# A spectral filter followed by a two-matmul block on one Trainium2 core: the table of issue order and engines is laid out anew

## The chip, the cores and the metric

The kernel runs on one core of a Trainium2 chip. Its time is the device time in microseconds of one execution; the time of a kernel is the median of several executions. Before the change it is 836.34 us, the median of three runs (835.13 to 836.74).

## The reference

```python
X = np.fft.rfft(x, axis=1)                  # x: 8 x 3008 x 256
Yr = Xr @ w_r - Xi @ w_i + b_r              # 256 x 256 weights
Yi = Xr @ w_i + Xi @ w_r + b_i
Yr, Yi = soft_threshold(Yr, 0.01), soft_threshold(Yi, 0.01)
y = np.fft.irfft(Yr + 1j * Yi, n=3008, axis=1)

h = y.reshape(24064, 256) @ w_in            # 256 x 2048
g = s * np.maximum(h, 0) ** 2 + b
out = g @ w_out                             # 2048 x 256
```

## The kernel before

The Fourier transform of 3008 = 94 x 32 points is done as two smaller transforms by matmuls. For each batch there are these steps, each a list of small units that are strewn between the matmuls of the second block:

- `s1_units`: the transform of length 94 (input `x16`, loaded by POOL in `load_x_later`, L360). The result `u` leaves PSUM by ACT or DVE (L301) and is written to a scratch tensor in HBM by the SyncE queue (SP, L796), and read back in another layout as `us` (`take_rows`, L812).
- `s23_units`: `fwd_unit` (transform of length 32, result `xf`), `sum_unit` (`s`) and `mix_unit` (the weights, result into `ring`, L889), then `shrink`: three DVE operations for the soft threshold (L908, L912, L916) and four moves on SP that bring the two halves of the partitions together (`ring<-ring`, L927; for the last units of a batch they are DVE copies, L933). `inv_unit` multiplies the moved `ring` by `T_t`; its result `v` is written to HBM (L964) and read back as `vs` in four loads of 384 KB (`take_half`, L981).
- `s4_units`: the last transform of length 94, into `yt`.

The second block runs over 48 tiles of at most 512 tokens. `first_mm` multiplies `yt` by `w_in` into PSUM (`psh`), 16 chunks of the 2048 columns for each tile. Two chunks at a time, ACT or DVE makes `relu` (`rt`, L1140 or L1142) and `square` (`gt`, L1151 or L1153). While a tile's first product runs, the tile before it gets its second one: `seven_mms`, a 2 x 2 block product with seven products in place of eight, into `psa`, or `second_mms` (plain) for the first four and last two tiles and those that are not full. The seven products need sums of the blocks of `gt`, in two halves q of the chunks: `s_op` with n = 1, 3 and 2 on DVE (L1303) and n = 4, `a12 = a12 + a11`, either on DVE (L1303) or as a transfer that POOL issues and that adds on its way (`gt<-gt`, L1295). DVE gathers the results (L1368) into `ost`, and SP sends them out (L1177).

What is not a matmul is recorded as a piece, in the order in which the program makes it. All 2681 pieces of the main part have an entry in the string `TURNS`: two base-36 digits make a number; its remainder by 4 is the engine (ACT, DVE, SP, POOL), its quotient a shift. `plan_turns` sorts the pieces by their place plus this shift, and `pump`, which runs ahead of each matmul, issues them in that order. So the table sets the engine of each piece and the order of each of the four queues. Each queue works its instructions strictly in that order. The order of the matmuls is not in the table: it follows from the calls.

```python
at = [divmod(int(TURNS[k : k + 2], 36), 4) for k in range(0, len(TURNS), 2)]
queue.extend(
    (k, ("act", "dve", "sp", "pool")[at[k][1]])
    for k in sorted(range(len(at)), key=lambda k: k + at[k][0])
)
```

Of the kernel before, what the change touches and what calls it, by code (L numbers as in the profile page):

```python
# [23 lines left out]


TURNS = (
    "24253220251x20281w262d1p29303a1o2942465i421c1t19181c211l181s1t34141t1w1g2p4b571b470r4310141s"
    "1930141o28191m221015191d1l1l1s2024301s2l1t2121292u3a2u26102d181l1p292l2x4u3m3u2q0w2o1h2m1q0s"
    "141h143w1d1x2d2d3u2i2y5e0o0x151p21293q2y4u220c2s0k0t10291o3k41111d1h2l5i4y46320812111c3w0x46"
    "162x0k0p0x191d1t3y1u422a08103s210k3q0p0s2o590s210p3q111h1x2p3u2q3a3u0c0g1s0l11151x212956463u"  # L30
    "2y0h0w1k2d2q3u051u0k1g1s0t2l0o6i1d1x292l463i2u2y0w1s0j370d0w1l0x1g381d1h1p1x3226362a0w321018"
    "2w3h4y5m3m4u0t15151l31213h39002y0h0g310p0x151h391p1h1l0c2i0g0g2t1c2i1g1s1h1x2y242c2x363a3e3e"
    "181g191m3a323u5a0x20113e0x10112c101g2c1d222m1c1m19291s241p21251w2k1w221s291t264e292l1s2k1p1v"
    "1s2w251l1o23251p1s2x1t21211q1w241x24242p21213m1x1w2h1t211s2d2m3q1k1o1x1k1s3a242o1t1y261c2p31"
    "1h1h3k1t1c1s2x3l242d1g2t1t191a1v1x1c2g1t1w1w2529351w2821291r731t1w281t2p1o1x1x2u2a1u4u1h212d"
    "2t4m4y5a360s1g140v5f1c1s111u2e12160p1h1l1x0t0w3k151r141t141o1p151t292h313i463q2u1b190s1t141h"
    "1o1t1c2x1p1o281p1s1n7f1t252l1s1w353h1p5e4a1h1p1x2h3i2m4y460o0w0x12101g0x2u1q0s212l103x143c0p"
    "130t1s3c1t110s101v1x1h2l142h1g761h1p292d2l2y3q3e2u1c25104614182c15181t184918201p39153i1x263e"
    "19181l15182x1c1k1w1h1m2u0z47212h1531393t4e4u3u4a0o280x0w4a104e0z0w1o0x0p0s131h151c1g281l191g"
    "1x1h252h2t4x31314d4d2t3p3p0o6q1d1m0k0w0l1d0s10281h491l561m2m1u0k0u0k2h0p1p1y1c241h221q2y2214"  # L40
    "252t1d1c2c1t1c1q3m3m2h2o320s241l0x2t1h18211p1d1k2h264m282e1k201l2120281x2d241p3i361l1s1t221o"
    "241l1u2q2d31191h3k251g2b1k1s3o291l1s2b211k1o2p1t1x201u1x341s20242w1t211u1x1w1x2s292x1p294e4m"
    "1h1k2c1h4a2e1g281d1i1m252x1d2s1h1g253p1c1p1g2s210x0y231t212k1o1x212l1o241x2125242c2121252d2h"
    "323q2i363b8319181c1s1h1p142p213m2y2e52150w1o0z5r191l1k201h3i2a2i1e151d1h253e263i3y152h0o1428"
    "1p0k2l1z0p0s2w1p0l0s2v1t18291c2d1l2h2l353y3a463e151c5i1828181c1h183c1d176r1d1h1g201h1p1g1t4y"
    "1s251h1s1l1t212d2y2i422u181i1g200p2m0s2h3918450t381d111r1414202l1p192p142b211h2l2x353a3u423a"
    "0o5y1024151e1h0w141w181h1p2q1s281h1p1p1x212h2t453l493135393d3h0w0w3o0x1p0w1m0f4z0l0u0g5i0k2x"
    "0o181k2c1p2u1d1m2l311d1d6e1k3c1h141e3i3q1f1c1g1o1p111s221j191h2g1s1l1t2h1o3e1u4e1o291l1o1t1k"
    "1w252h1g1q1h3m1o2g1t1s211p2i1k1u292p2438251d1c271s2030291t1t2b211k212t1w25251u202l1x20202c1x"
    "204e291x1w2c212p1p292u1k1p2k1k1q1y1o251p22292l1s3k211s3123282h1g391x1l1e1z211g2c1x1w1x24242x"  # L50
    "242g1t1x1z631t2c341p1x1o1x1x3u1t1x292h322m3i3u101w150z4v141s113a15291t290x1c2s0x1b1g251k301x"
    "1d1x29393t4e4i4u3q1719101x141d1d21181c1d1g201l1k1b5r251h251g201d1x294i1t21292l3m4m2q2y101819"
    "3m181o151e101x2h1545181s0x1b1d2445291p1c1t23291o1x1o201t3y1t1x21252p2y3e3m46141g143a1c1o2s15"
    "141d1h351c1t1d391c222h2m1h1g1s1l242l1p242c213m1n4j292p1p3d3p414m564q3y182c0p0o0y0x1a0v0w2419"
    "0t0w1b1t15141o2c1x1h1k341p1x252h2x4d4p3t31253l290s160w3m0w1w0x151c1d1l2x391l1y1446101o101l2q"
    "202k1p1y1c2h2x1o1h381p1o1y3q3u3d2d4e142l1h111n1d14201l1d1g2h2a1i282e1g201h21242o21291w1x3a1w"
    "2d1x2i1s2g1p1u2p311k1p3h1x1o231o1w38251p1s271x1o1w2s1w1x251u21291w24242g25251u252821292p351s"
    "25321o1o201p2u1u1w281l1u2h2l243g1l1p2l3p242l1g2t1t1h1a1v1x1g241t20212p2c2p1s241p1p3j7b211o20"
    "2h2p1k1p1x5e1h2d2l2p3q2u3y2y0o1c0w0r57141k113610291p2h0x14280t1714211c2o1t0x1t2d2x2x4a3e3m2u"
    "13150w2h0x1d142x181g1h1o28211o1j5n291x2h1s201t1x2h4y1t292h2l2u323i4i10140x4e141k112m101l2p18"  # L60
    "1p1g2x0l1319283g1x15181g1z2d1w211s2h1w3u1t1t252d2l3q2q3a3q181o1852141k2h151d1h1g351k2019211k"
    "3q252e1l1k1s1h1x31251o241l1u1j4f292l1l2p353h3u424m460w2811104e0w3y0z0w1s150t0s171p11181k281t"
    "1d1g391l1t252l354h3135412t353x0s3a0w160s140p1910141x2x3d193m141i181w1c1t1y242o1t221g2l311s1l"
    "2s1t1s263m3q1n2s2y1c241p193d1l1c1p211d1k2o2e461k1u1k2c1l1x1x241x25281t3a1s2d1t221o2c1l222p31"
    "1k1t401t1s231o282w251p1g2b1x1o1s2s1t1x211u253c1s21202c1x201u291x1w2s1x212a1w1w291x2q5u1w251t"
    "1u1w251w2921251o2h461s1s1t1s1x1w2h1s201p1r7r1p563q3a1i2q1m1k2w111h0w151d1l21292u3m2a460o210w"
    "0r57181s152q1q141l1t29111c3c1h1z1c211g1w1x1h252t31353q423246130t0w1g0x151h2l1c1g1l1o2g1l1w1j"
    "7b1p1x2920281p1x2d4i1t1t212t3i2u3i4a141g181i191k1d36101p291c351c3k0p17191s2t211d141h23211g2t"
    "1g311o661t1t1x253d4i563y4i101w145m14181k15191p1929181o0x29143u111a11181o191l2d211o241926174j"
    "2d2p1h3d3p454m52424m1c3c0l0o1q0x1a0v0w1g190t0w1b1t1514183k1x1h1k1w1p252d2t3x3d452x413p2x210p"  # L70
    "1e0s120o280x1d14182w192d1p4i195q1c2d1o1p2e242g1h1q1c2d2t1o1h341l1k1y3e3m1f2k2u142g1h111l1d14"
    "2w2p191d1p224i2c2m1g2g1h1p1t2o21291g1t221o2h1x261w2k1l1y2p2t1o243o1l1p1v1w202g291t1t2b211k21"
    "2s1w25251u21301w2120291x1w3i211s21342h3h1o1p2y1l1k1s1h261m1l241t262d2l20341p2o2x1r1o251o3121"
    "1l1e232121301x1w2021202h1w2g1t1t21252c252p1s212p3i1t1x2d2x42323e42101c141g1s1d1i191p2d2x1l1k"
    "2o1h1v1g2d1o2c251h252h31394e3a3m3q1f1d1k1s141d1d1h1k251h1k241l1o2d1x2h1s241x2l21261x292p4t5e"
    "5q5u4m181g1h221c1w191e1c1t291g3d1k200x1719182g1h151d1f1p182514381l1t212d314i4q3i2y101c1d3i1c"
    "1o1919211d1l1c1s25351d1q1h1o201p1x2d20281p3a2d2l1t2l31394m3i463m141k0t141i0v1k201l151g1r1p1x"
    "1o251t1s202821252d2h2t2l3d2t2h3p352x242i0s100p150w2c1h2h253i142d1h282e1o201l262h311p1s2s1p1w"
    "2a3a3q1n1k2k1x1d1z1p1s281p1t21223e1w251x251w21292t1x221k1w242h1t222p311s203w1x1k231o282w251p"
    "1g27291t1k2k1o1x1x292l1t202c3d1t1s21251w2k1w1x2y1s1s2d1p2q1w2d1l1u1w2g20202125242524242h463e"  # L80
    "4a2m2a361d1g191l1c1x1g1w1h321i21291o34191n1s2l211p271t1s2821252c202d1x212429212l29361s1s1x20"
    "212a292l1s2g1h2t1s30211l271x1o20212125242o2121202k1x1x21361x2021241x262h2p1w301h1r1w2x211p27"
    "1x1o2c1x1w2k202p1x1x1w212h2m1s1x1w21292a1w24252524252425242l213e2i22262q2e1c29191t1k291w243d"
    "3m3a21251o281d1n1o2p1t1h2x1l1k291p1w2c1w2d1t2124252p2u1w211t1w253a1o21202120291w2o1t1y1w2021"
    "25242425282126292a1x2e2122"
)


# [1466 lines left out]
```

## Time and profile before

| | |
|---|---|
| median of 3 runs | 836.34 us |
| the profiled execution's own time | 833.63 us |
| its span, first to last instruction | 831.7 us |
| PE (matmul) busy | 808.9 us, 97% |
| DVE busy | 748.0 us, 90% |
| ACT busy | 742.7 us, 89% |
| POOL busy (it issues transfers) | 114.0 us, 14% |
| transfers issued by SP (queue q1) | 82.12 MB, 35.2% of the 16 DMA engines' time |
| transfers issued by POOL (queue q0) | 32.19 MB, 24.4% |

The profile names an instruction by its line, its engine and the tiles that it writes and reads. An idle time of an engine is put down to what ended it: `PE psa L238 <- DMA gt<-gt` is idle time of PE ahead of a matmul into `psa` that a transfer `gt<-gt` ended. All matmuls stand under L238, the helper that issues them.

### The profile page before, as it was taken

Reading aid. Unit: us, or ns where it says so; the run is one execution under the profiler, and the core shown is the slowest. Engines: PE = TensorE matmul, PEld = TensorE weight load, DVE = VectorE, ACT = ScalarE, POOL = GpSimd, SP = SyncE. Lnnn points to the kernel's source line nnn. Section 1 sums busy time; section 2 is a strip of 40 time slices with the busy share of each in tenths; the row PEclk is TensorE's granted clock in tenths of the full one; section 3 lists DMA queues with packets and bytes.
Section 4 is the critical chain, followed back from the end, with each engine's and each line's share of the span. In section 5 each row is a group of like instructions: output and inputs, shape, how many; then the busy total and the mean of one; then the engine's idle time right before and its main releaser. Section 6 shows DMA issues by size and latency. Waiting matters only on the chain.

```text
span 831.7 us, 21177 instructions
## 1 busy us (share of the span) xinstructions
PE 808.9 (97%) x8526; PEld 599.1 (72%) x8526; DVE 748.0 (90%) x1290; ACT 742.7 (89%) x941; POOL 114.0 (14%) x156
## 2 busy tenths in 40 slices
PE   8999999999999899999999999999999999999997
PEld 7857767767677666777667776777767777767765
DVE  5988989989999798999989999899999999889893
ACT  5989989989999898999989999999998999788773
POOL 4531000211002010121000210111101001000000
PEclk9999999999999999999999999999999999999999
DMA  8955445668665678568674776745786346522312
GB/s 202 183 146 112 118 141 155 137 128 150 182 161 119 134 165 219 141 130 175 157 186 92 132 173 194 186 108 116 170 217 152 78 115 143 137 70 53 76 46 64
DMA packets 124516, 115.66 MB, mean 139 GB/s; under 512 B 12150, under 2 KB 101754, under 8 KB 124418
## 3 DMA queue, kind: packets, MB, share of 16 engines
q1 hardware_dynamic: 103906, 82.12, 35.2%
q0 software_dynamic: 20512, 32.19, 24.4%
q8 instruction: 67, 1.10, 0.6%
q14 instruction: 31, 0.25, 0.1%
HBM read 53.52 MB, written 46.66 MB: 120 GB/s over the span
## 4 chain that ended last, share of the span: by engine, by line
PE 43%; DVE 4%; DMA 2%; issue 1%; ACT 0%; DVEq 0%
PE psh L238 19%; PE psa L238 15%; PE psf L238 9%; DMA gt<-gt 2%; DVE ost L1368 1%; DVE gt L1303 1%; DVE ring L933 0%; DVE s L1303 0%; DVE rt L1142 0%; DVE gt L1153 0%; DVE v L301 0%; DVE ring L916 0%; DVE u L301 0%; ACT gt L1151 0%; ACT rt L1140 0%
## 5 line engine op out<-in xcount | busy, mean ns | idle before, releaser
L238 PEld LDWEIGHTS <-gt 128*128 128x128 f16 (+1 forms) x4272 | 310.3, 101 | 165.1 <-DMA gt<-gt 6.2
L238 PE MATMUL psh<-yt,w_in 128*128 128x512 f16 (+1 forms) x1344 | 398.1, 378 | 1.1 <-ACT u L301 0.8
L1140 ACT ACTIVATE rt<-psh 128x1024 f32<-128x1024 f32 (+2 forms) x330 | 331.7, 1008 | 38.0 <-PE psh L238 35.8
L1151 ACT ACTIVATE gt<-rt 128x1024 f16<-128x1024 f32 (+2 forms) x275 | 284.4, 1047 | 10.2 <-DVE rt L1142 7.8
L238 PE MATMUL psa<-w_out_t,gt 128*128 128x128 f16 (+3 forms) x2224 | 215.1, 229 | 6.2 <-DMA gt<-gt 5.6
L238 PEld LDWEIGHTS <-w_in 128*128 128x128 f16 x1536 | 132.3, 98 | 27.4 <-issue 7.3
L1295 POOL DMA_DIRECT2D gt<-gt x68 | 61.1, 899 | 597.4 <-DVE s L1303 149.6
L1153 DVE TENSOR_TENSOR gt<-rt 128x1024 f16<-128x1024 f32 (+2 forms) x109 | 128.6, 1188 | 3.5 <-ACT rt L1140 2.4
L238 PE MATMUL psa<-T_s,gt 128*128 128x128 f16 (+1 forms) x1680 | 128.5, 219 | 0.4 <-DVE gt L1303 0.3
L1142 DVE TENSOR_SCALAR rt<-psh 128x1024 f32<-128x1024 f32 (+2 forms) x54 | 64.9, 1202 | 11.9 <-PE psh L238 11.1
L1368 DVE SCALAR_TENSOR_TENSOR ost<-psa,s_bc,bias_bc 128x256 f32<-128x256 f32 (+1 forms) x140 | 67.0, 479 | 6.8 <-PE psa L238 6.0
L889 DVE TENSOR_TENSOR ring<-psf,s 128x512 f16<-128x512 f32 x84 | 57.7, 687 | 11.1 <-PE psf L238 4.1
L1368 DVE SCALAR_TENSOR_TENSOR ost<-psa,s_bc,ost 128x256 f32<-128x256 f32 (+1 forms) x117 | 56.0, 478 | 6.6 <-PE psa L238 5.9
L1303 DVE TENSOR_TENSOR gt<-gt 128x1024 f16<-128x1024 f16 (+1 forms) x88 | 59.9, 680 | 0.5
L1303 DVE TENSOR_TENSOR gt<-gt,s 128x1024 f16<-128x1024 f16 (+1 forms) x78 | 53.3, 683 | 1.8 <-PE psa L238 0.9
L1303 DVE TENSOR_TENSOR s<-gt 128x1024 f16<-128x1024 f16 (+1 forms) x78 | 53.1, 681 | 1.5 <-ACT gt L1151 0.8
L238 PEld LDWEIGHTS <-s 128*128 128x128 f16 (+1 forms) x624 | 41.8, 100 | 17.4
L238 PE MATMUL psh<-tail,w_in 128*128 128x512 f16 (+1 forms) x192 | 52.1, 352 | 0.2 <-ACT rt L1140 0.2
L238 PE MATMUL psf<-W_g,xf 128*128 128x256 f16 x336 | 50.4, 273 | 0.0
L238 PE MATMUL psa<-T_s,s 128*128 128x128 f16 (+1 forms) x624 | 47.5, 219 | 0.0
L238 PEld LDWEIGHTS <-xf 128*128 128x128 f16 x504 | 45.0, 98 | 3.3
L301 ACT CAST yt<-psf 128x480 f16<-128x480 f32 (+3 forms) x66 | 35.1, 540 | 7.5 <-PE psf L238 6.5
(114 smaller groups left out, 885.1 us busy)
## 6 DMA issues: line engine op xcount, KB each, us to landing
out_dram<-ost SPq DMA_DIRECT2D x65, 256.0 KB
gt<-gt POOLq DMA_DIRECT2D x64, 256.0 KB, 5.1
ud<-u SPq DMA_DIRECT2D x56, 192.0 KB
us<-ud SPq DMA_DIRECT2D x28, 384.0 KB
vd<-v SPq DMA_DIRECT2D x42, 256.0 KB
vs<-vd SPq DMA_DIRECT2D x28, 384.0 KB
x<-in_x_dram POOLq DMA_DIRECT2D x56, 188.0 KB, 5.9
ring<-ring SPq DMA_DIRECT2D x120, 64.0 KB
```

Source lines behind the costliest of these rows:

```text
L238: return nc.tensor.matmul(out, lhs, rhs, **how)
L301: (nc.scalar.copy if e == "act" else nc.vector.tensor_copy)(out=dst, in_=src)
L889: lambda e: nc.vector.tensor_tensor(out=ring[0][:, i % 4], in0=ps, in1=hold[i // 2][:, i % 2].unsqueeze(1).to_broadcast([P, 2, D]), op=ALU ...
L1140: nc.scalar.activation(out=rt, in_=ps[:, :, 0:w], func=AF.Relu)
L1142: nc.vector.tensor_scalar(out=rt, in0=ps[:, :, 0:w], scalar1=0.0, scalar2=None, op0=ALU.max)
L1151: nc.scalar.activation(out=gt, in_=rr, func=AF.Square)
L1153: nc.vector.tensor_tensor(out=gt, in0=rr, in1=rr, op=ALU.mult)
L1295: nc.gpsimd.dma_start(out=a12, in_=a11, accum_op=ALU.add)
L1303: nc.vector.tensor_tensor(out=out, in0=a, in1=b, op=op)
L1368: ins = nc.vector.scalar_tensor_tensor(out=out(), in0=hold[of], scalar=s_bc[0:size], in1=other(), op0=ALU.mult, op1=ALU.add,)
```

## The change

All 59 lines of the string `TURNS` are replaced; the code is the same. The author's words: the table is laid out anew with transfers that share in two queues by a weight for each kind, and with margins.

```diff
 TURNS = (
-    "24253220251x20281w262d1p29303a1o2942465i421c1t19181c211l181s1t34141t1w1g2p4b571b470r4310141s"
-    "1930141o28191m221015191d1l1l1s2024301s2l1t2121292u3a2u26102d181l1p292l2x4u3m3u2q0w2o1h2m1q0s"
...
+    "28292i242d21282g242e2k1x292g2m1s2l3a3m3y321h251g1k1o251t1k24252w1c242g1t313r5f1v5j1f2v211l1l"
+    "1s351c1x311h1u22181w211c1p1w2c211s301t1x1x21252l2q3m2u32143c1c1l1p1x2d2x4e4m2u3i101o153e2m0w"
...
 )
```

Read by the rule of `plan_turns`, the two tables give the pieces to the engines as follows; the pieces themselves, what each needs and the 8526 matmuls are the same.

| pieces | before | after |
|---|---|---|
| sums n = 4 (`s_op`) that could go to either | 68 POOL, 10 DVE | 57 POOL, 21 DVE |
| relu and square (`first_mm`) | 605 ACT, 163 DVE | 601 ACT, 167 DVE |
| `xf` out of PSUM (`fwd_unit`) | 54 ACT, 30 DVE | 64 ACT, 20 DVE |
| `v` out of PSUM (`inv_unit`) | 49 ACT, 35 DVE | 58 ACT, 26 DVE |
| `s` out of PSUM (`sum_unit`) | 34 ACT, 8 DVE | 27 ACT, 15 DVE |
| all pieces | 878 ACT, 1217 DVE, 470 SP, 116 POOL | 885 ACT, 1221 DVE, 470 SP, 105 POOL |

Of the sums n = 4, 13 go from POOL to DVE and 2 from DVE to POOL. Many more pieces change their engine both ways (88 of relu and square go from DVE to ACT, 92 from ACT to DVE), and in all four queues pieces move by some places.

More of the change, by code (lines that the diff above doesn't have):

```diff
@@ L26 @@
 TURNS = (
-    "24253220251x20281w262d1p29303a1o2942465i421c1t19181c211l181s1t34141t1w1g2p4b571b470r4310141s"
-    "1930141o28191m221015191d1l1l1s2024301s2l1t2121292u3a2u26102d181l1p292l2x4u3m3u2q0w2o1h2m1q0s"
-    "141h143w1d1x2d2d3u2i2y5e0o0x151p21293q2y4u220c2s0k0t10291o3k41111d1h2l5i4y46320812111c3w0x46"
-    "162x0k0p0x191d1t3y1u422a08103s210k3q0p0s2o590s210p3q111h1x2p3u2q3a3u0c0g1s0l11151x212956463u"
-    "2y0h0w1k2d2q3u051u0k1g1s0t2l0o6i1d1x292l463i2u2y0w1s0j370d0w1l0x1g381d1h1p1x3226362a0w321018"
@@ L32 @@
[L32 to L85, printed above, removed]
+    "28292i242d21282g242e2k1x292g2m1s2l3a3m3y321h251g1k1o251t1k24252w1c242g1t313r5f1v5j1f2v211l1l"
+    "1s351c1x311h1u22181w211c1p1w2c211s301t1x1x21252l2q3m2u32143c1c1l1p1x2d2x4e4m2u3i101o153e2m0w"
@@ new lines @@
+    "1d1h1w3g1d1p1x2d424e2y360o111921252l3q5e4a2a0g240p0o193114283p1d1h1l212a56362q0s7i111o2c1d36"
+    "2q250k1515292h3h4m3y4q3e0c102c210t1e0w1g4c5h0w2h0t12191p212p364y2q3q0p0g180o15191p1t2x4m4u42"
+    "2u0g0o1k1p2i320t160t1s381039103a1d1h25353m4a3y320x2k0n370o0s1h0x1g381d1t212p3m3q2y2m0t3q1018"
+    "4o21563e4i3m0p151l212d4d353d004u0k0o140p11191h2l2d1t350s1a110o201p32212o1p1s1y1x2o294a3m3m2i"
+    "181o1p1y363q3e5e19211p1y14151420141k1x2p462u1w261g291k1w1h25241s2120261w281x4e4m292d1w3c1l1v"
@@ new lines @@
+    "1w2p211p1p271t1k1o3d1s1x211u20281x25242p21244621202c253p1s2d4y3e1p1o1w1l1t4e1s241h1q2m1d292l"
+    "191s3s1x1d1s2935242h1g391x1d1623211o2c2121282c2531282g1x212343212c3k1t311s1x1x421y2i221h1p2t"
+    "313q3a4q3q0s1p180v5z1c1w193u1a323y102d1t2l11142c113j141h14241t151x2t2x3t564i463q171918201515"
+    "183h181l1p1g201l1k1b7r1l212h1k2019311t5u261t21252l4e2y4m2i101g142m1c1p192u2i142d2x1g3p0w1c0x"
+    "1b192434251d141c271x1k2t1s301t3q1t1x25292l4i3q2i2y142d182y1d1c2c1d1g1x1k311t28213l1o1y2l3m42"
@@ new lines @@
+    "1l1o1w1p1x2l1s202c1l2i1u1f572h2x1p2d2t313q4e323q142g0t143y184y0z143k1l11101r1x1d141g251l1k1w"
+    "291x2h2x35453d4p3d49313t3l0w120s160w1c0x191c1g3p151l1x5e2m4u1u105y0w1t1g1s1y1o281p262m1q221c"
+    "212d1h1k2k1p1o1y3q3q4d2o2y14211h11491d1c1w1c1d1h1t2y32212a1k1s1h1p1w2s1x2h1w214a3e1s21292e1s"
+    "2c1p2y262l2t1c2030191h1r1w2d3g2h1x1o2x291s1w2x1x251s1u25342024242c21213y2121252g31351s1t3a4y"
+    "1k1p1s1k3i321k20191i26252d1o3g192c2p1j1o21202w251d1q351x212g1w21212h24301t2429203k2121292d2h"
@@ new lines @@
+    "3i2m2u3m1b6v1x181c301p2l141p252m3y424m15142k177v1h1t1g251d222y1m16151t3d3t4y3y4e4y192d0k0k1c"
+    "110s2x1b0x141w1p0x103d1p101t182d1l2p313d464i3a3i150o5i0o180w1s3h141o11136v1h1p1g1s1x491d1p2a"
+    "1k1x1o241t1t1x2l323m3a3y1c1m1c20111q152p3d141l1o2c1p191z1k2k3k2p1t1l2t1k2j291p2d31313i423q2y"
+    "0w3y0w2c181i1h151c251g1p1w4i1s24251p2p21252h2t493l453p3h2x2l310s0w1c454l0w1m0f5j15360h0m0k2h"
+    "101w1c1w1p1y192a293d1k1o2i202w211g1q464e1z1k1s2k1x19203q3h1l1p211s1l1s1x1o1y2q4m1g2p1l1k1x20"
@@ new lines @@
+    "281x2h292i1t3a1o241s2128212y1o1y2d2t1p3s291o1s2f1w202g291x1w4h2121202k1x21251y252o2021202s1x"
+    "1x4e1x1x1w2o2p351l1t2y1x1k2p1h1y1q1w2c1l222h2p203x1x242p1v2c2p1s2s251p1i27251o2c2128292s2435"
+    "202g1x1x1z7f252c2o1p2l1o1x1x3y1t21292l4i3i2m3q1g251g135b181s151q142t1t2t19182k1l1z1829182821"
+    "15212h2x3t4q4y463q1b19181k151h1t2d1g1k1l1k2d1h1s1f7n1l202d1k201p2x2d461t1x252t4q2y3m2y102814"
+    "3m141c151e152l391g4d111c1l1z15243c2d1p10182b291k1t202t1c4m1p1p21313h3q464y4a1k1w141e1c1d2c1d"
@@ new lines @@
+    "1c1l1c1l1c241t2l1d7i1x2e1h202o1g1x3d1w1x28212a1n4b292l1l2p393h4u4e423i101o0p0w4i144i0r1k2w0x"
+    "110s0z1l111g0w1p1d1c1w2k1l1t212l4d413p3h3t312h2h0s521h1u10200p150w102l193p1d3a1g4e1w2g1g1p1y"
+    "1k2c1h1u1h2h2x1h203c1p1w26424a2l205u1c2g1p0x2h1l1c2w1w1h1l2d2m4i1g1m1c301d1x1w281t311o1p1y1p"
+    "1x1w221s281t2e2l2x1x243s291p2f1s1w2g291x1w2b291x292x1w29281y242s2124242h21214u2d2020292p2x1t"
+    "25321o1o2l1o2y2m1k1w1h1m2h2x1o2w1p1s2539282h1k39211h5u1z1x1w241t21202h202t1w281t251v7f2d1s28"
@@ new lines @@
+    "1t291o1x2l2q1t1x2t314i3m323q10181d0z5b181w151i181x1x2h191c201p231c29202c211l292d2p353e3m3u3y"
+    "1b0x1g21101d1k411k2c1l1k251l241j7n29202920281h1x2h4u1t1x292l363u3a2m182g181m181t151e1c293d1o"
+    "2l1o2s151n1p1o342d1x1l1k2f251s2x1o2g1t4q1t1t21293h3q524a4m1o25181i1h1g1s1d1g1l1l351g1w1l3p18"
+    "1y1h3m1h1k1s1l1x2d2k1s2g1p1y1n4v2h311x2h2t4l5u5e4y4i1g3c0x0w161c1m131o2d1l19101n1p1514181s1t"
+    "1h1s2c1p1x2d2p3p39314d354d3x2p0k620t1i0w1c0x1919181x293h1t46182q182k181c1u1g2g1l1y1h2l351p1w"
@@ new lines @@
+    "2w1t1h1q3q3y1r2w361g2p1t191x1p1g2h1k1l1s242a4e2c2m1w251t291w28292h1t252a1s25242a202d212e2p2x"
+    "1w203k1x1w23202c3s291x1o2b291x1o2o21291w1y212s2025282x1x213y2121212k1w2h2y1s1s2c1p1y261t253l"
+    "3m20241x2121251w251y202g1x1w292k2t20341x1z8b1x262m26322m4e18341d2l1c1l1l1t292d2m3m3y320w2518"
+    "0z531c1w191m3618351t2l191c2g1h1z1c291g28210x212p2x3t424i464q1b19182015151t1t141o1p1s2d1h1w1j"
+    "7n1h1s251s242h2p1p3e1t212h354a4m3m2y1024142u141l1116142l391h3x101c1l1z1524302d1p101c2b211k2h"
@@ new lines @@
+    "1k2p1p461t252h2p2x324u424a141o182y141o3o15181h1k2t1k20191p1d1q2l2q1h1k2s1p213120212c252e1r4n"
+    "2h311p2h393t424a4u4e141s11144m184a0v1k24190x0w1b1h15141l2c1x1g1g281l252d2l2x3d4l3l4141352l0l"
+    "2a1g1m0w280t1d0w18211h3h2l3e1k1q1w2o181x2y1s2k1p1u1l2l2p1t24391t282i3i4e1n2x361k2c1p1d3d1h1g"
+    "2c1g1l1o212y4a1s221s2l1h1x1w281x2d2c1x3e1s2120261w2c1x2a2t311p24391p1x1z20203h291x1w2b2d1s20"
+    "2t20212022242c2429282l2529222h24242h2531202h2u1w1w241t3y1y282c1x222l2p243o1p1p351r282h1k3921"
@@ new lines @@
+    "1l1e23251o2c2121282l242l20281x292d242g29311w252h5e1x212h2p3y4a322m141k181k241h2i1g2d212h151k"
+    "2s15491k251o2k1x1h212t2x3d3i424e3m1b1d1g1s1519183l1g2c1d1g1x1h1k1x202d202g1p2d214e252d2l2p2y"
+    "4a3a4e1c1k193a1k20151y1c2h2x1k450x2k193t19182s251h18271x21251g2o1x212h3d414m4u563y101s18561d"
+    "1k1d1h1h1s3l181o151t193i19181l1c1k1x1g1w1h322d311l2h313d4e3u3e4a102k0p144213181o1p15141r1p1x"
+    "1o2c1t1s1t2821292d2l3d49312t3l2d2d212k2y0w140x15142w1t291t461g251s2d2m1w2g1t2e2l391k1l2s1x1o"
@@ new lines @@
+    "22363q1v1g2w211l3d1x1o1s1t1x21222a1w312125242c2121252e242h242g21262h3521283k251o2b1w2c3d291l"
+    "1o4d211s1w2p1t1x1x1w2c1w20292s1x20251w202t1x2h2m1w1w2g1t4q2025292a1w2g202021252425242l213e3i"
+    "2e1y222i1c2119251k2g1w2d1x2i262h2t1w2o1x23202o291t2t251w2c21212h242c2129282l25252l2u1w202124"
+    "252i2h2t202o1p23202o291t39251w2c212125242o2121242d212h292e1w2d2428292e2h2p24341p351w24251p2b"
+    "211s2g21242g242t212524253l3q1w2d1w1x2d2m1o1s1t211s202529282p252e3e2u2y2a221g2d1d1x1o2d20283p"
@@ L86 @@
+    "3y4225291s2p1h1r1s2c1t1l2h1l1k2d1p1s2h242c212928293h3m202120241x22202c1x1w1x2429282d2i212c20"
+    "2c2528292c252a292q252e2122"
 )
```

## The prediction

> **What bounds the kernel now.** I read the busy times by stretch first, then what PE waited for, then the places of the long waits, then the two queues there. Columns of the first: stretch, its length, then PE, weight loads, DVE, ACT and POOL, each busy us (instructions), granted clock, DMA share, GB/s.
>
> ```profile
> 0.00:44.80 44.80, 40.10 (x503) 34.22 (x504) 34.29 (x73) 33.92 (x64) 23.01 (x37) 1.00 0.92 194
> 44.80:820.00 775.20, 762.03 (x7965) 559.38 (x7966) 710.93 (x1213) 707.74 (x876) 90.96 (x120) 1.00 0.59 137
> 820.00:831.70 11.70, 6.72 (x60) 5.53 (x58) 2.74 (x5) 1.06 (x1) 0.00 (x0) 0.91 0.26 69
> ```
> ```profile
> 260.00:280.00 20.00, 17.74 (x179) 13.15 (x177) 15.91 (x31) 17.11 (x23) 3.46 (x5) 0.91 0.60 116
> 280.00:300.00 20.00, 20.00 (x208) 14.79 (x207) 19.75 (x36) 19.14 (x26) 2.82 (x4) 1.00 0.69 148
> 300.00:320.00 20.00, 17.75 (x176) 11.71 (x174) 17.29 (x33) 16.81 (x23) 2.27 (x3) 1.00 0.85 208
> ```
> ```profile
> 276.50:279.90 3.40, 3.12 (x17) 1.97 (x17) 2.47 (x4) 2.12 (x4) 0.00 (x0) 0.50 0.27 67
> ```
>
> PE sets the time: from 44.8 us, where the table begins to rule, to 820 us it idles 775.20 - 762.03 = 13.2 us. Its matmuls are the same after the change, so this idle time is nearly all that a new order can win. One stretch more costs: from 276.5 to 279.9 the clock stands at 0.50, and the 3.12 us that PE worked there would have taken half, 1.5 us. What PE waited for (us, times, longest):
>
> ```profile
> PE psa L238 <- DMA gt<-gt: 5.6, 3, 2.0
> PE psf L238 <- DMA ring<-ring: 3.7, 2, 2.3
> ```
> ```profile
> 276.78 0.37 PE L238 MATMUL psf<-ring,T_t 128*128 128x256 f16 x1 [2.26 <-DMA ring<-ring]
> ```
> ```profile
> 318.86 0.34 PE L238 MATMUL psa<-w_out_t,gt 128*128 128x128 f16 x3 [1.75 <-DMA gt<-gt]
> ```
> ```profile
> 714.50 0.34 PE L238 MATMUL psa<-w_out_t,gt 128*128 128x128 f16 x3 [1.90 <-DMA gt<-gt]
> ```
>
> So five waits make 9.3 of the 13.2 us: three for a sum n = 4 that POOL sent (318.9, 420.4 and 714.5 us), two for moves of `ring` (1.39 us at 172.0, 2.26 at 276.8). With the slow clock behind the longest they cost 5.6 + 3.7 + 1.5 = 10.8 us. The other 3.9 us are waits of under 0.8 us.
>
> Why the sums come late (start, length, what):
>
> ```profile
> 309.59 0.86 POOL L1295 DMA_DIRECT2D gt<-gt  x1 [0.92 <-DVE ost L1368]
> ```
> ```profile
> 310.59 2.90 SPq L981 DMA_DIRECT2D vs<-vd  x3
> ```
>
> A sum on POOL lands 5.1 us (median) after its issue, 3.2 to 9.2 in all. The one of 309.59 us took 9.2, that of 411.34 us 9.0, that of 705.97 us 8.5: the three late ones. Each has three or four loads of `vs` (384 KB each) issued by SP within 3 us of it. The moves of `ring`, at 262 to 270 us on the SP queue:
>
> ```profile
> 261.50 2.62 SPq L1177 DMA_DIRECT2D out_dram<-ost  x4
> 264.79 0.66 SPq L927 DMA_DIRECT2D ring<-ring  x1
> 265.49 1.63 SPq L1177 DMA_DIRECT2D out_dram<-ost  x2
> 267.17 2.73 SPq L927 DMA_DIRECT2D ring<-ring  x3
> ```
>
> One of four moves goes out as soon as its input is there; the others stand behind two stores, the last is issued at 268.6 us, and by then POOL has issued two sums and three loads of x (266.97 to 269.14). The packets between 268 and 277 us, by queue (packets, MB, share of the 16 engines):
>
> ```profile
> q0 software_dynamic: 623, 1.10, 79.3%
> q1 hardware_dynamic: 856, 0.45, 21.0%
> ```
>
> By count queue 1 moved more packets, but POOL's are larger and took four fifths of the time. The last move needed some 8 us, until POOL's transfers were through.
>
> **The change, part by part.** The matmuls and their order are the same in both programs; numbers of buffers alone differ. The rest I read from the two tables, piece by piece.
>
> *The three late sums.* All three are among the 13 that go from POOL to DVE. On DVE such a sum takes 0.68 us (L1303). Between the piece that frees it and itself the new DVE order has 6, 4 and 5 instructions, by their rows 4.7, 2.6 and 3.6 us; with its own 0.68 and a room of 9.9, 9.7 and 9.2 us ahead of the matmul, 4.5, 6.4 and 4.9 us are left. The waits go: -5.6 us. DVE has room there: busy 17.3, 17.8 and 17.2 of 20 us in the stretches from 300, 400 and 700 us. For the other ten the room left is 1.4 to 9.3 us. The two sums that go to POOL have 11.4 and 8.7 us from their input to their matmul, against the median of 5.1.
>
> *The moves of `ring`.* At 276.8 us the new SP order has the eight stores first and then the four moves in one row. The eight take 5.1 us by their rows and can begin at 260.1 (two wait for data until 261.5), so the moves go out at about 265.9 to 268.0 in place of 264.8 to 268.6. Three are ahead of POOL's transfers, whose packets begin at 268.5 us, and the sum of 268.57 us is no longer among these. At 172.0 us three moves go out ahead of two stores that were ahead of them; the last is issued at 164.5 in place of 165.6. The waits were 2.26 and 1.39 us. Bounds: nothing (the last move still lies behind POOL) to -5.2 us with the clock. I take all of it: with three moves through, the last has 6 us for its 128 packets of 512 bytes, and queue 1 moved 856 in 9 us, 95 each us, even beside POOL.
>
> *Work added.* By the counts and row means: on DVE 11 sums (+7.5 us) and 4 of relu or square (+4.8), 7 `s` (+4.8), less 10 `xf` (-6.9) and 9 `v` (-6.2), with the few others about +5 us; on ACT about +2 us. PE hides it where an engine has room. It has none from 280 to 300 us (19.75 and 19.14 of 20). From 260 to 300 us DVE is busy 35.7 us; the pieces whose input falls in it carry 2.0 us more in the new table, while PE would pass in 40 - 3.8 = 36.2 us. DVE is overbooked by 1.5 us, part of which can slide behind 300 us: 0 to +1.5, I take +0.7. In the same stretch of the other batches DVE and ACT are as full (19.1 to 19.9 from 380, 480, 580 and 680 us), and PE lost nothing there.
>
> *New late pieces.* 2681 pieces are set anew. What this adds can't be read off: 0 to +5.2 us (two waits like those for `ring`, with the clock), I take +0.8. I laid the SP rows end to end in the new order: of the 40 groups of four moves 10 are issued over 0.7 us later against their matmul. The shortest lead is 3.5 us (3.4 before, and PE didn't wait for that one); one group, needed at 681.0 us, falls from 5.5 to 3.6. Two sums that stay on DVE move back 16 and 12 places and, counted as above, have 0.3 and -0.1 us left ahead of their matmuls at 226.3 and 227.1 us. The loads of `vs` keep 5.4 us at least; alone in the queue one took 3.0 to 3.9.
>
> A new wait of 2 us may cost more than itself: by the Trainium skill ("TensorE: Matmul & The Clock Gate", Part 1) the clock gate looks at a free-running window of 3413 ns, so an idle time halves the clock or not by where it falls. The trace agrees so far: 2.26 us was followed by 3.4 us at 0.50, waits of 1.75 to 1.99 by none.
>
> **The sum.** -5.6 - 5.2 + 0.7 + 0.8 = -9.3 us. The profiled execution took 833.63 us (span 831.7 and 1.9 around it), so it would become 824.3; the median of the runs is 836.34, 2.7 above it, and I forecast 836.3 - 9.3 = 827.0 us.
>
> **The rivals.**
>
> *The moves of `ring` wait as before* (B). Queue 0 still has the loads of x and a sum at 268 to 276 us, and the last move goes turn for turn with them until they are through; being issued 0.6 us sooner doesn't help. For it: the 79% to 21% above. Against: only one of four moves is left to meet them. Then 836.3 - 5.6 + 0.7 + 0.8 = 832.2 us. The Trainium skill speaks for this ("DMA: Bandwidth & Descriptors", section on queues, rings and completion order): each engine takes turns between queues packet by packet, and taking one of several transfers out of the other queue changes nothing while others are left in it; the trace's 623 against 856 packets agree with turns.
>
> *New groups of moves come late* (C), the case on the other side. The new SP order puts stores ahead of moves at ten places. A late group costs 1.4 us, or 3.8 with the slow clock, 2.6 on average. Three new ones leave 834.8, four 837.4 (no change), five give 827.0 + 13.0 = 840.0 us: from the fifth on it is slower. For it: POOL's bursts recur in every batch. Against: in before only two of 40 groups were late, and the leads laid out above.
>
> *What is won goes to DVE* (D). The moves wait as in B, and the DVE work of +4.7 us by the five counts stands wholly on PE's path (0.7 of it is counted): 832.2 + 4.0 = 836.2 us, no change. For it: both engines are over 95% busy in the second half of each batch. Against: the sums that move stand in stretches with over 2 us of room.
>
> **How the numbers follow.** Forecast 0.64 (its own range 823 to 831), B 0.18, C 0.12, D 0.06. Within 0.2% (834.7 to 838.0) is about what a measurement of this kernel can't tell from no change. Faster: 0.64 + 0.18 = 0.82; same: D, 0.06; slower: C, 0.12. The range goes from 822.8 (if nothing comes back, 836.3 - 10.8 = 825.5, and most of the 3.9 us of short waits go too) to 836.3, which takes in B and D and leaves out C.
>
> **What would show it.** Right: the waits of PE for `gt<-gt` are gone or under 1 us; those for `ring<-ring` under 1 us; the clock is 1.00 between 44.8 and 820 us; PE idles some 4 to 6 us there; `gt<-gt` on POOL is x57. Wrong: a wait for `ring<-ring`, `vs` or `us` of over 1 us at a new place; PE waiting for DVE in 280 to 302 us by more than 1.5 us; a stretch at clock 0.50.

## The result, and the profile after

The changed kernel takes 823.14 us (median of 4 runs, 822.59 to 823.85). Four runs of the kernel before beside them gave 836.54 us: a ratio of 0.984 (95% interval 0.982 to 0.986), 13.4 us less. Later, beside 15 runs of before (835.17 us), it gave 823.71 us: 0.9858 (0.9824 to 0.9892), 11.5 us less. The profiled executions, 833.63 and 822.59 us, lie 11.0 us apart, their spans 10.9. (Of the four executions of one experiment, `e5_three_back`, the profiled one has a granted clock of 0.94; its median and its ratio leave that one out.)

The busy times of the changed kernel by stretch, with the columns of the prediction's first fence:

```profile
0.00:44.80 44.80, 39.46 (x503) 33.50 (x503) 34.12 (x73) 33.69 (x64) 24.60 (x39) 1.00 0.94 193
44.80:809.00 764.20, 760.58 (x7973) 559.37 (x7973) 715.35 (x1219) 708.19 (x885) 79.20 (x107) 1.00 0.58 135
809.00:820.80 11.80, 5.63 (x50) 4.81 (x50) 1.72 (x3) 0.42 (x1) 0.00 (x0) 0.85 0.26 69
```

In the long stretch PE idles 764.20 - 760.58 = 3.6 us in place of 13.2, 9.6 less; and no stretch at half clock is left there, which is 1.5 more. That is 11.1 us, and the spans differ by 10.9: the waits of PE and the half clock account for the gain.

What PE waited for in the changed kernel (us, times, longest), the three of the list that the prediction bears on:

```profile
PE psm L238 <- DMA x<-in_x_dram: 2.7, 8, 0.7
PE psf L238 <- DVE v L301: 1.5, 4, 0.8
...
PE psf L238 <- DMA ring<-ring: 0.6, 1, 0.6
```

The first belongs to the start, which both kernels have. The waits for `gt<-gt` are gone. Of those for `ring<-ring` 0.55 us is left, at one place. The groups of the sums n = 4 in the changed kernel (busy us and mean ns of one behind the bar):

```profile
L1303 DVE TENSOR_TENSOR gt<-gt 128x1024 f16<-128x1024 f16 (+1 forms) x99 | 67.4, 681 | 0.5
...
L1295 POOL DMA_DIRECT2D gt<-gt x57 | 51.3, 906 | 598.2 <-ACT rt L1140 91.3
```

POOL sends 57 sums in place of 68. A sum on DVE takes 0.68 us, as before.

The moves of `ring` at 260 to 275 us in the changed kernel's timeline (start, length, what), first SP, then POOL, then PE:

```profile
258.36 5.24 SPq L1177 DMA_DIRECT2D out_dram<-ost  x8
266.53 8.41 SPq L927 DMA_DIRECT2D ring<-ring  x8
```
```profile
263.71 0.89 POOL L1295 DMA_DIRECT2D gt<-gt  x1 [16.04 <-PE psf L238]
264.28 1.91 POOL L360 DMA_DIRECT2D x<-in_x_dram  x3
```
```profile
273.23 0.38 PE L238 MATMUL psf<-ring,T_t 128*128 128x256 f16 x2 [0.55 <-DMA ring<-ring]
...
298.28 0.38 PE L238 MATMUL psf<-ring,T_t 128*128 128x256 f16 x2 [0.78 <-DVE v L301]
```

The eight stores do stand in one row ahead of the moves. But there are three empty microseconds behind them, from 263.6 to 266.53: SP waits for DVE, whose last operation of `shrink` (L916) ends at 266.5, later than before (264.7). First this operation before, then in the changed kernel:

```profile
264.04 0.69 DVE L916 TENSOR_TENSOR ring<-ring 128x1024 f16<-128x1024 f16 x1
```
```profile
265.78 0.69 DVE L916 TENSOR_TENSOR ring<-ring 128x1024 f16<-128x1024 f16 x1
```

POOL's transfers, on the other hand, begin at 263.7 in place of 267.0. So all four moves go out behind them, and yet PE hardly waits. Why, the experiments had to tell.

### The profile page after: what moved, and what is told of

Same layout as the page of the kernel before. It is cut to its first block, busy times and chain, and to the rows that moved or that the text cites. A ratio compares the mean times of both kernels' runs of the same rounds, so it can differ in the third digit from the quotient of the medians.

```text
span 820.8 us, 21151 instructions
## 1 busy us (share of the span) xinstructions
PE 805.7 (98%) x8526; PEld 597.7 (73%) x8526; DVE 751.2 (92%) x1294; ACT 742.3 (90%) x948; POOL 103.8 (13%) x145
## 4 chain that ended last, share of the span: by engine, by line
PE 89%; DVE 6%; DMA 2%; ACT 2%; issue 1%; POOL 0%; SPq 0%; DVEq 0%; ACTq 0%; POOLq 0%
PE psh L238 37%; PE psa L238 32%; PE psf L238 19%; DMA x<-in_x_dram 1%; PE psm L238 1%; DVE gt L1153 1%; DVE v L301 1%; DVE ost L1368 1%; DMA ring<-ring 1%; DVE ring L933 1%; POOL x L376 0%; DVE rt L1142 0%; DVE u L301 0%; DVE z L661 0%; ACT gt L1151 0%
## 5 line engine op out<-in xcount | busy, mean ns | idle before, releaser
L1140 ACT ACTIVATE rt<-psh 128x1024 f32<-128x1024 f32 (+2 forms) x334 | 336.7, 1010 | 34.7 <-PE psh L238 32.2
L1151 ACT ACTIVATE gt<-rt 128x1024 f16<-128x1024 f32 (+2 forms) x267 | 275.2, 1046 | 5.9 <-DVE rt L1142 3.6
L1153 DVE TENSOR_TENSOR gt<-rt 128x1024 f16<-128x1024 f32 (+2 forms) x117 | 138.7, 1193 | 8.6 <-ACT rt L1140 8.0
L1295 POOL DMA_DIRECT2D gt<-gt x57 | 51.3, 906 | 598.2 <-ACT rt L1140 91.3
L1142 DVE TENSOR_SCALAR rt<-psh 128x1024 f32<-128x1024 f32 (+2 forms) x50 | 59.6, 1192 | 9.4 <-PE psh L238 8.4
L1303 DVE TENSOR_TENSOR gt<-gt 128x1024 f16<-128x1024 f16 (+1 forms) x99 | 67.4, 681 | 0.5
L301 ACT CAST u<-psf 96x512 f16<-96x512 f32 x74 | 42.7, 583 | 0.7 <-PE psf L238 0.5
```

The source lines that it names most:

```text
L301: (nc.scalar.copy if e == "act" else nc.vector.tensor_copy)(out=dst, in_=src)
L1140: nc.scalar.activation(out=rt, in_=ps[:, :, 0:w], func=AF.Relu)
L1142: nc.vector.tensor_scalar(out=rt, in0=ps[:, :, 0:w], scalar1=0.0, scalar2=None, op0=ALU.max)
L1151: nc.scalar.activation(out=gt, in_=rr, func=AF.Square)
L1153: nc.vector.tensor_tensor(out=gt, in0=rr, in1=rr, op=ALU.mult)
L1295: nc.gpsimd.dma_start(out=a12, in_=a11, accum_op=ALU.add)
```

## The experiments

A piece is named by its place in the order in which the program makes the pieces; the diffs show its engine or its queue's order as the two digits of `TURNS` decode to. All medians in us; the ratio is to runs of before on the same chip, taken beside them.

| kernel | from | median (runs) | ratio, 95% interval |
|---|---|---|---|
| e1_three_sums | before | 827.97 (6) | 0.9903 (0.9877 to 0.993) |
| e2_sp_order | before | 833.12 (12) | 0.9984 (0.996 to 1.0008) |
| e3_one_sum | before | 833.35 (12) | 0.9985 (0.9964 to 1.0007) |
| e4_sums_and_order | before | 827.65 (6) | 0.9913 (0.9885 to 0.9942) |
| e6_with_pool_order | before | 822.58 (6) | 0.9871 (0.9843 to 0.9899) |
| e9_loads_later | before | 836.35 (10) | 1.0007 (0.9984 to 1.0031) |
| e10_changed_again | the changed kernel | 823.71 (4) | 0.9858 (0.9824 to 0.9892) |
| e5_three_back | the changed kernel | 826.02 (3) | 0.9908 (0.9873 to 0.9943) |
| e11_three_back_again | the changed kernel | 826.62 (6) | 0.9906 (0.9875 to 0.9936) |
| e7_one_sum_back | the changed kernel | 826.23 (4) | 0.9905 (0.9876 to 0.9934) |
| e8_sp_order_back | the changed kernel | 824.06 (4) | 0.9881 (0.9851 to 0.991) |

**The three late sums alone.**

```diff
-994, 1356, 2400: POOL, behind 959, 1266 and 2395
+994, 1356, 2400: DVE, behind 1008, 1361 and 2411 (their places in the changed table)
```

(In the changed table 1362 stands between 1361 and 1356; in this kernel it is on ACT.)

> The kernel before with one thing of the change: the three sums that came late (needed at 318.9, 420.4 and 714.5 us) go from POOL to DVE, at the places which the new table gives them; all else as before. If each wait has its own cause: PE's waits for gt<-gt of 5.6 us vanish, those for ring<-ring (3.7 us) and the stretch at half clock stay: 5 to 6 us less than before. If DVE has no room and gives it back: 0 to 3 us less, and PE waits for DVE near 319, 420 or 714 us by over 1 us each.

Measured: 827.97 beside 834.97 us for 23 runs of before, 7.0 us less. No wait for `gt<-gt` is left; the one for the moves is:

```profile
PE psf L238 <- DMA ring<-ring: 4.0, 2, 2.7
```

So the three sums win what the waits cost (5.6 us), and a little more than the 5 to 6 us expected. Where the rest comes from is seen at the third experiment.

**The order of SP alone, at the two places of the moves.**

```diff
 SP at 157 to 167 us (stores, and the moves 415 to 418)
-409 408 407 429 430 427 418 428 410 415 416 417
+408 410 409 428 407 416 415 418 429 417 427 430
 SP at 260 to 270 us (stores, and the moves 819 to 822)
-799 798 814 797 812 813 820 811 800 819 821 822
+797 814 813 811 798 799 812 800 820 821 819 822
```

> The kernel before with the new order of the SP queue at two places alone: the stores and moves of ring issued at 157 to 167 us, and those at 260 to 270 us (there all eight stores ahead of the four moves). Theory of the prediction, that the moves are late by their place in the SP queue: both waits for ring<-ring (1.4 and 2.3 us) go, and the half clock: 3.5 to 5.2 us less. Rival, that moves issued while POOL's queue is full don't get through until it is empty, wherever they stand: the wait at 276.8 us stays at 1.5 us or more; that at 172 us may change by the 1.1 us of earlier issue: 0 to 1.5 us less.

Measured: 833.12, which can't be told from before. The waits for `ring<-ring` are gone, both, but a new one has come. First PE's list of the second kernel, then DVE at that place (start, length, what, and in brackets the idle time ahead of it):

```profile
PE psa L238 <- DVE ost L1368: 3.9, 3, 3.6
```
```profile
175.70 0.48 DVE L1368 SCALAR_TENSOR_TENSOR ost<-psa,s_bc,bias_bc 128x256 f32<-128x256 f32 x1 [4.71 <-DMA out_dram<-ost]
```

The two stores that are now last in the row (427 and 430) are issued at 165.3 to 167.0 us, amid POOL's transfers (a sum at 164.60, a load at 165.17, a sum at 166.39, two loads from 166.95). They get through late, DVE waits 4.71 us for the buffer of `ost`, and PE 3.6 us for DVE, with half clock behind it (176.3 to 179.7 us). The moves were helped and the stores paid: an order of one queue is right only together with the order of the other.

**One sum fewer in POOL's queue, without a new order of SP.**

```diff
-838: POOL, behind the load 787
+838: DVE, behind 843
```

> The kernel before with the one sum that POOL issues at 268.6 us moved to DVE; the SP queue as before. Theory of the prediction (place in the SP queue): the wait at 276.8 us stays near 2.3 us, no change beyond 1 us. Rival (the moves wait until POOL's queue is through): that queue ends 256 KB, by its rate of some 150 KB a us 1.7 us, earlier; the wait falls to about 0.6 us and the half clock goes: 1.7 to 3.3 us less.

Measured: 833.35, which can't be told from before; in the profile the wait for the moves is as long as it was:

```profile
PE psa L238 <- DMA gt<-gt: 6.5, 3, 2.6
PE psf L238 <- DMA ring<-ring: 3.7, 2, 2.2
```

In before, then, the place of the moves in SP's queue counts, and one sum less does not. The first line holds something else. The same three waits as in before's profile come to 6.5 us in place of 5.6 (1.46, 2.64 and 2.42), and behind the two long ones the clock is at half (the columns are those of the stretches, the clock is the third number from the end):

```profile
421.80:425.20 3.40, 3.40 (x22) 2.21 (x21) 2.30 (x3) 1.05 (x2) 0.00 (x0) 0.50 0.04 11
718.80:722.20 3.40, 3.40 (x29) 2.69 (x27) 3.33 (x5) 1.59 (x3) 0.00 (x0) 0.50 0.37 99
```

A third such stretch stands behind the 2.19 us for the moves (278.5 to 281.9 us). This profiled execution took 838.51 us, the median of the same kernel is 833.35. All the runs of before scatter from 831.8 to 839.4 us, those of the changed kernel from 822.6 to 823.9. The granted clock of the whole run goes with it: 0.988 to 0.991 in the four slowest runs of before (838.8 us and more), 0.996 to 1.000 in the ten fastest (832.8 and less), 0.997 to 1.000 in the changed kernel; one stretch of 3.4 us at half clock lowers it by 0.002. So a wait of 2 us or more costs itself or up to 1.8 times as much, by chance; with such waits the scatter goes.

**Both together.** The diffs of the first three kernels in one.

> The kernel before with the three parts together: the three late sums and the one of 268.6 us on DVE, and the new SP order at the two places; some 30 entries of 2681. Theory, that these waits are the gain and that the rest of the new table is worth little: 9 to 11 us less than before, within 3 us of the changed kernel. Rival, that the rest of the new table matters (shorter waits everywhere, or DVE's new order): 7 us less or fewer, 5 us or more above the changed kernel.

Measured: 827.65; the waits for `gt<-gt` and `ring<-ring` are gone, and the wait of e2_sp_order is there again:

```profile
PE psa L238 <- DVE ost L1368: 3.4, 3, 3.0
```

It comes to no more than the three sums alone: the rival's time, but not its reason. (Behind this wait of 3.0 us the clock stays at full, unlike in e2_sp_order.) The changed kernel has the same order of SP there and has no such wait. The difference is in POOL's queue: there the load 398 is ahead of the sum 439 and out long before, and 439 stands behind 454, whose input comes late. So POOL's transfers begin at 166.6 us, in place of 165.4 in this kernel, when the stores are nearly out.

**The same with POOL's order at that place.**

```diff
 POOL at 164 to 168 us (439 and 454 are sums, the others loads of x)
-439 398 454 423 469
+398 454 439 423 469
```

> The fourth kernel (four sums on DVE and the new order of SP in two places) and, besides, the new order of POOL at 160 to 168 us: sum 439 behind 398 and 454 in place of ahead of them. Theory (the wait at 176 us comes from two stores that are stuck behind POOL's transfers, and the changed kernel is spared it because POOL waits for 454's input there): the wait of PE for ost at 176 us is gone and with it 3.0 us and 1.7 of half clock: 822 to 824.5 us, the changed kernel's time within 0.2%, by 33 of 2681 entries. Rival (the rest of the new table is worth something of its own): 826 us or more, with the waits at other places, or the wait at 176 us stays.

Measured: 822.58 us. The wait is gone, and no wait between 60 and 809 us is over 0.35. The ratio and that of the changed kernel can't be told apart. So 29 pieces of 2681 (a closer count than the 33 above), 4 sums, 24 of SP and one of POOL, give all that the new table gives, as far as these ratios tell (within some 3 us). In the string that is 66 numbers, as the shifts of neighbours change with them; the new table changes 2352.

**Sums on POOL, with the loads of `vs` elsewhere.** First the three sums back on POOL in the changed kernel:

```diff
-994, 1356, 2400: DVE
+994, 1356, 2400: POOL, right behind their input
```

> The changed kernel with one thing undone: the three sums that came late (pieces 994, 1356, 2400) go back from DVE to POOL, right behind their input; DVE is 2.0 us emptier. Theory (in the changed kernel, too, these three pay by themselves): their waits for gt<-gt come back, three of 1.8 to 2.6 us, perhaps one or two with a stretch at half clock: +5.6 to +8 us, so 828.7 to 831 us. Rival (the order of the rest leaves the POOL sums time enough, or the room on DVE is what counted): no wait over 1 us for gt<-gt, and 821 to 824 us.

Measured: 826.02 (825.38 to 828.44), less than expected. Its profile, the one at the lower clock, has one wait for `gt<-gt`, not three. So it ran once more:

> The changed kernel with the three sums back on POOL, once more, for a profile at full clock (the first had 0.95 all through). Theory now, from the first profile: the new order of SP has put the loads of vs 2.9 us and more behind two of the three sums, which land in 4 to 5 us; only the third (needed at 714 us) lands after 8.4 us, with a wait of 1.7 to 2.3 us: 825 to 827 us. Rival (at full clock PE is earlier, and all three are late): three waits, 828.7 us or more.

Measured: 826.62 beside the changed kernel's 823.71 beside the same runs of before, 2.9 more. From the new profile's list:

```profile
PE psa L238 <- DMA gt<-gt: 2.5, 1, 2.5
```

and at the place of that wait POOL's sum and SP's loads:

```profile
697.32 0.86 POOL L1295 DMA_DIRECT2D gt<-gt  x1 [1.47 <-ACT rt L1140]
```
```profile
697.13 2.02 SPq L981 DMA_DIRECT2D vs<-vd  x4
```

The third sum goes out together with four loads of `vs` and lands after 9.1 us. At the other two the changed order of SP issues the loads 2.8 and 3.2 us behind the sum; these land after 4.0 and 4.9 us, in time. So the new table has removed two of the three waits twice over. The reverse test, in before, leaves the sums where they are and puts the loads off:

```diff
 SP at 309 to 317 us (984, 985, 1004: loads of vs; the others stores of u)
-993 963 984 985 1004 1016 1003 978
+993 963 1016 1003 984 985 1004 978
 SP at 411 to 417 us
-1365 1347 1348 1364 1367 1351
+1367 1351 1347 1348 1364 1365
```

> The kernel before with one thing changed: at two of the three late sums (318.9 and 420.4 us) the loads of vs that SP issues within 3 us of the sum go behind the two stores of vd that followed them, some 5 us later; the sums stay on POOL, at their places. Theory (the loads of vs are what makes these sums land after 9 us): both sums land in 4 to 6 us, PE's waits for gt<-gt at 318.9 (1.75 us) and 420.4 (2.0 us) are gone, the one at 714.5 us (1.9 us) stays; 830 to 832 us, 3.7 us less than before in one profile, less or more by the half clock. Rival (the sums are slow by themselves, by gt's own state or by POOL's queue): the three waits stay and the time is that of before; or the later loads make PE wait for vs at 321.5 and 422.3 us.

(The stores that the loads go behind are of `ud`, not of `vd`.) Measured: 836.35, as before. In the profile:

```profile
PE psf L238 <- DMA ring<-ring: 4.5, 3, 2.7
PE psf L238 <- DMA vs<-vd: 4.4, 2, 2.8
...
PE psa L238 <- DMA gt<-gt: 1.7, 1, 1.7
```

The two sums now land after 5.5 and 3.9 us in place of 9.2 and 9.0, and their waits are gone; the one at the untouched place stays. The cause of these two is shown. (The waits for the moves of `ring`, the first line, are those of before, and one of 0.42 us.) But the loads are late in their turn, by 2.8 and 1.6 us: the theory is right on the cause, the rival's second half on the time, and putting the loads off pays nothing.

**What sets the moves of `ring` in the changed kernel.** One sum back into POOL's queue, and, apart from it, two stores back to their place between the moves:

```diff
-838: DVE
+838: POOL, between the loads 787 and 863
```

> The changed kernel with sum 838 back on POOL, between the loads of x at 264 to 266 us (256 KB more in queue 0, about 1.7 us of its time). Theory (where the moves of ring go out after POOL's transfers have begun, as they do in the changed kernel at 266.5 us, the length of queue 0 sets when they land): the wait for ring<-ring at 273 us grows from 0.55 to about 2 us, with or without half clock: 824.5 to 827 us. Rival (only the place in SP's queue counts, or the moves take turns with queue 0): the wait stays under 1 us and the time within 0.2% of the changed kernel.

```diff
 SP at 258 to 271 us (811 and 800 are stores, 819 to 822 the moves)
-797 814 813 811 798 799 812 800 820 821 819 822
+797 814 813 798 799 812 820 811 800 821 819 822
```

> The changed kernel with two of its twelve pieces on SP at 260 to 270 us put back as they were before: two stores behind the first of the four moves of ring, so that the last three moves go out about 1.7 us later, at 269 to 271 us. Theory 'place in SP's queue': the last move lands 1.5 us later, the wait for ring<-ring at 273 us grows from 0.55 to 1.5 to 2.3 us: 824.5 to 827 us. Rival 'queue 0 sets it': the moves carry nothing until queue 0 is through at 271.5 us in any case, so the wait stays at 0.5 to 0.9 us and the time within 0.2% of the changed kernel.

Measured: 826.23 and 824.06, beside 834.49 for before. (The changed kernel did not run beside these two; by the ratios they lie at 0.9905 and 0.9881, it at 0.984 and 0.9858.) With the sum back the wait is

```profile
PE psf L238 <- DMA ring<-ring: 2.0, 1, 2.0
```

and with the stores back there is none, though the last move is issued 2 us later than in the changed kernel; the largest wait there is now 0.65 us, for `ost`. Between the span with the sum back, 823.6 us, and the changed kernel's lie 2.8; 1.45 are this wait, and 0.9 fall in the first 64 us, where the two are the same. The wait of the changed kernel itself scatters, 0.55 and 1.26 in its two profiles and 1.00 at this place in e11_three_back_again, so the sum is worth 0.7 to 1.5 us. So here it is POOL's queue that counts and not the place. Eight profiles together, in us; POOL's burst is from the first to the last packet of 1 KB or more in its queue, PE's arrival is the start of the matmul less its wait:

| kernel | last move issued | POOL's burst | PE arrives | wait |
|---|---|---|---|---|
| before | 268.6 | 268.5 to 276.9 | 274.5 | 2.26 |
| e3_one_sum | 269.1 | 269.0 to 276.3 | 275.0 | 2.19 |
| e2_sp_order | 272.1 | 272.6 to 281.5 | 278.4 | none |
| e6_with_pool_order | 266.2 | 266.8 to 273.5 | 272.6 | none |
| changed | 268.7 | 265.2 to 271.9 | 272.7 | 0.55 |
| e10_changed_again | 269.3 | 265.6 to 273.3 | 273.1 | 1.26 |
| e7_one_sum_back | 269.9 | 266.2 to 274.8 | 273.7 | 2.00 |
| e8_sp_order_back | 270.7 | 265.5 to 271.2 | 273.8 | none |

Where the last move is issued ahead of the burst's first packet, PE doesn't wait, however long the burst is. Where it isn't, PE either comes after the burst (e8_sp_order_back) or waits until between 0.1 us ahead of the burst's last packet and 1.3 us behind it, whatever the place of the moves. The five other profiles agree at this place, but for 1.4 in place of 1.3. At 172 us only the first half holds: in all thirteen profiles PE waits just where the last move is issued behind the burst's first packet, but these waits (before and three others) end 1.2 to 1.7 us ahead of its last. Why a shorter burst didn't shorten the wait in e3_one_sum (its burst ends 0.6 us sooner, its wait ends 0.4 us later) stays open.

**The changed kernel once more.**

> The changed kernel, once more beside the others of this call: 822.5 to 824 us by every theory. What it tells: how far a single profile of it scatters (PE's waits of over 0.5 us between 44.8 and 809 us should again be two, at 273 for ring and at 298 us for v, as nothing in it is near the point where the clock halves).

Measured: 823.42 to 823.90. The waits are at the places named, at 274.4 us 1.26 in place of 0.55, and at 299.4 us 0.8 (a third one of 0.8, at 45.5 us, every kernel here has).

## Why the prediction was right, and where not

Forecast were 836.3 - 9.3 = 827.0 us; measured are 823.1 and 823.7, at the low end of the forecast's own 823 to 831. The direction and what bounds the kernel were right; by the steps:

*What bounds the kernel.* Right. The gain is idle time of PE and the half clock, 9.6 + 1.5 us, and the 8526 matmuls are the same. Of the signs named, the clock and the 57 sums are as said; PE idles 3.6 and 4.7 us in the two profiles, for 4 to 6; the wait for the moves is 0.55 and 1.26 us, once over the 1 us allowed.

*The three late sums, -5.6 us.* Right: the waits are gone, and alone they win 7.0 us by medians (by the interval of the ratio 5.8 to 10.3). The cause, loads of `vs` issued within 3 us, is shown for the first two by e9_loads_later; that the third is late with the loads beside it, and the first two are in time without them, e11_three_back_again shows. What the step didn't see is that the new SP order takes the loads away from two of them as well: in the changed kernel the move to DVE is worth only 2.9 us.

*The moves of `ring`, -5.2 us.* The size was nearly right, 3.7 + 1.5 - 0.55 = 4.65, or 3.9 in the second profile; the step that failed is "Three are ahead of POOL's transfers". I laid SP's rows end to end and took the input of the moves and the start of POOL's transfers from before's profile, 264.7 and 268.5 us. In the changed kernel DVE ends `shrink` at 266.46 and POOL's packets begin at 265.2: all four moves are behind. What saved the wait is what the step named in half a sentence, that the sum of 268.57 us is no longer there. It shortens the burst from 8.6 us (e7_one_sum_back, from the table) to 6.7 and 7.7 (the two profiles of the changed kernel), and the burst begins 3.3 us sooner than in before while PE comes 1.8 us sooner. That the term came out at nearly its size is thus in part luck, since the place in SP's row, from which it was reckoned, didn't do it. So B's mechanism, that the last move lands only when POOL's transfers are through, was right for the changed kernel, and its price wrong; and its reason that taking out one of several transfers changes nothing holds in before (e3) and not in the changed kernel (e7).

The rule of the Trainium skill behind it ("DMA: Bandwidth & Descriptors", section on queues, rings and completion order), turns packet by packet, may fit one trace and doesn't fit the other. The packets by queue (packets, MB, share of the 16 engines), of e7_one_sum_back from 268 to 273 us:

```profile
q0 software_dynamic: 341, 0.60, 85.7%
q1 hardware_dynamic: 240, 0.11, 10.9%
```

and of the changed kernel from 266 to 270 us, where queue 1 has no line:

```profile
q0 software_dynamic: 266, 0.46, 94.3%
```

There the moves are issued from 266.53 on; at 255.61 us, with POOL's queue empty, the first packets of such moves came 1.3 us behind the issue. Here none comes until 270. So it is in e8_sp_order_back (none from 266.9 to 269.5 us), e11_three_back_again (none from 266.5 to 270.3) and e5_three_back (none from 273 to 277), with moves issued meanwhile. The first trace can be turns, though its counts don't show them: a packet is one row there, 512 bytes of a move or 2 KB of a POOL transfer. The second is not.

*Given back to DVE, +0.7, and new late pieces, +0.8.* Both too high. The waits of PE that are neither for sums nor for moves were 13.2 - 9.3 = 3.9 us and are 3.6 - 0.55 = 3.1: 0.8 less in place of 1.5 more. What was given back at 280 to 302 us is the wait of 0.78 at 298.28, where before had two of 0.33 and less. The two sums on DVE for which I had left 0.3 and -0.1 us, and the moves needed at 681.0 with a lead of 3.6, made no wait.

*From the profile to the median.* This step cost nearly as much: 2.7 us were added where 0.55 was measured. The terms were made against a profile of 833.63 us and give 824.3, 0.6 to 1.2 from the measured medians; I then added 2.7 us, because the median of before was higher. But the distance is not a constant around a kernel. By the runs it comes in good part from the very waits that the change removes: a wait of 2 us sometimes has 3.4 us of half clock behind it, and the profile of before had that once, the one of e3_one_sum three times. Without these waits the changed kernel's median is 0.55 above its profile. With the profile alone as base the forecast would have been 824.3. Besides, the median of three runs, 836.34, may itself have been high: 23, 11 and 15 later runs of before, on other chips, gave 834.97, 834.49 and 835.17.

*The rivals.* C, new late groups, did not come, though e2_sp_order and e4_sums_and_order show that it was near: with the new order of SP and the old one of POOL a wait of 3.0 to 3.6 us stands at 176 us. I had looked only for moves that come late, not for stores. D did not come: DVE has 3.2 us more to do (751.2 beside 748.0) and its one new wait of PE is 0.78 us. (The five counts of D come to +4.0 us, not +4.7; with that D would stand at 835.5, still no change.)

## What to carry to other kernels

Where several queues share the transfer engines, read an issue order across the queues: here a transfer that the critical engine needed soon was in time when it was issued before another queue's burst began, or when the burst was over before the need; moving it in its own queue alone handed the wait to a neighbour. When the bound engine is 97% busy and idles in few long waits, list them with their place and try the few entries that touch them; here 29 pieces of 2681 gave the whole gain. And look at the scatter of the runs before you add a profile's gain to a median: waits that halve the clock in some executions and not in others make the old kernel's median and scatter larger, and both go with the waits.

## What the runs showed of the hardware

- A transfer of POOL that adds to `gt` (256 KB) lands, at the three places of the late sums, after 3.8 to 5.5 us when no load of `vs` goes out within 2.8 us of it (e5_three_back, e9_loads_later, e11_three_back_again), and after 7.5 to 9.7 us when three or four go out, the first of them between 0.6 us ahead of it and 1.1 behind it (before, e2_sp_order, e3_one_sum and the same three).
- The half clock: waits of 2.2, 2.4 and 2.6 us in e3_one_sum and of 2.7 in e1_three_sums and e9_loads_later were followed by 3.4 us at 0.50; waits of 2.0 in e7_one_sum_back, 2.5 in e11_three_back_again, 2.8 in e9_loads_later and 3.0 in e4_sums_and_order by none. In every trace the stretches between two changes of the clock last whole multiples of 3.413 us (in before 269.65 and 549.55, 79 and 161 times). This fits the rule of the Trainium skill cited in the prediction ("TensorE: Matmul & The Clock Gate", Part 1), that the window runs by itself; the idle window of about 3.4 us that the same Part names for the half clock does not fit, as waits from 2.2 us were enough here. The half clock shows as a spread of some 7 us between executions of one kernel.
- With queue 0 full, queue 1 can move nothing for some 4 us (changed kernel, 266 to 270 us; e5_three_back, 273 to 277) or 240 packets in 5 us (e7_one_sum_back). What decides between the two is not known from these runs.
